# Longformer attention and a gated MLP on one core: later rounds in another unit order, with the second pair's key and query copies behind the first pair's scores

## The chip, the cores and the metric

The kernel runs on one core of one Trainium2 chip. The metric is the device time of the core in microseconds (us); lower is better. A core has the engines TensorE (PE; its weight loads appear as PEld), VectorE (DVE), ScalarE (ACT), GpSimd (POOL) and SyncE (SP, which here issues most of the DMAs). Each engine carries out its instructions in the order written in the program, and waits at an instruction until what that needs is there.

## The reference

Attention over 8 batches, 8 heads, 576 positions and 64 dimensions a head, with a band mask of 32 positions to either side and 8 global positions, which see everything and are seen by everything. The heads are laid side by side to 4608 rows of 512 and go through an MLP whose activation is h·cos(h).

```python
scores = scale * np.matmul(q, k.transpose(0, 1, 3, 2))
mask = np.abs(pos[:, None] - pos[None, :]) <= window        # window = 32
mask = mask | is_global[:, None] | is_global[None, :]
attn = softmax(np.where(mask, scores, -1e9))
x = np.matmul(attn, v)  # heads side by side: (4608, 512)
h = x @ w_in            # (512, 2048)
out = (h * np.cos(h)) @ w_out
```

## The kernel before

The work is cut into pairs of heads (32 pairs: 4 in each of 8 batches) and into half batches of two pairs. The half batch `s` has the pairs `2s` and `2s+1`. For a pair there are, in this order:

- copies: `local_k` (L607, DVE, tile `kw`) and `local_q` (L619, DVE, tile `qb`) spread keys and queries, which a transposing load has put into `kT` and `qT`, into 11 blocks with the room for the global positions in front. POOL fills that room (`globals_kq`, L579 and L586);
- scores: 22 matmuls on PE (L699, tile `st`), which read `kw` and `qb`; then four exponentials on ACT (L702 and L707, tile `e`) and three products with the mask on DVE (L703 and L708, tile `pm`);
- values: 22 matmuls (L719, into `pv`), then four small operations and the normalising product on DVE (L730, tile `xn`);
- turning: 6 transposes on PE (L744, tile `tx`) and two DVE operations, the second of which writes `xT`, the MLP's input; for the last pair of a batch POOL writes the global columns (L752).

The MLP goes over tiles of 512 rows, in units of four matmuls of 128x512 each. An in-unit (L762) makes one block of 128 hidden columns in a bank `ph` of PSUM (two banks take turns, tag "h"; scores use one of them too); ACT takes its cosine (L768) and DVE multiplies (L769), which frees the bank. An out-unit (L800) is a quarter of one output block; four of them fill the bank `po` (one bank, tag "o"), and then ACT or DVE in turn copies it out (L805 or L807) and SP stores it. A cosine and an exponential need different tables on ACT, so each change between them costs a table load (L702 and L768, ACT_TABLE_LOAD).

What stands between what is written out by hand, as strings of steps. A start-up list, `FRONT`, is followed by rounds `s` = 4 to 15, with lists of their own for rounds 4, 5 and 6 (`MID`, `FIFTH`, `SIXTH`), and `ORDER` for the nine rounds 7 to 15. The letters of a step:

- `s`, `p`, `x`: scores, values, turning; `k`, `q`: the copies. The second letter says of which pair: `a` and `z` are the first and second pair of this round's half batch, `c` and `d` the first and second pair of the next round's;
- `1`: an in-unit with its cosine and product; `2`: an out-unit;
- `n`: squares of the previous half batch's `xn` on ACT (L818), for a check of the range;
- `G`: on POOL, the global positions of the next half batch's pairs into `kw` and `qb`, then a copy of one element of this half's `xn` (L980, `gate`), which holds the queue, and then three DMAs that cast values, keys and queries of half batch `s+2` (L268 and L272).

```python
for step in {4: MID, 5: FIFTH, 6: SIXTH}.get(s, ORDER).split():
    if step == "1":
        one()
    elif step == "2":
        two()
    ...
    else:
        f, pr = (STEPS | OTHER)[step[0]], 2 * s + "azcd".index(step[1])
        if pr < B * NP:
            f(pr, *[int(x) for x in step[2:]])
```

At a round's end SP is given the loads for half batch `s+2`: two transposing DMAs into `kT[s % 2]` and `qT[s % 2]` (L284 and L285), and the values. After the last round a tail runs the in- and out-units that are left, one of each in turn. `kw` and `qb` have four buffers each, one per pair, `kT` and `qT` two, one per half batch.

Of the kernel before, what the change touches and what calls it, by code (L numbers as in the profile page):

```python
# [23 lines left out]
G = 8  # L24
# [20 lines left out]
TT = 512  # L45
NTT = NT // TT

ORDER = "sa 2 2 2 2 sz pa 1 1 2 xa pz G 1 1 2 xz n 1 1 2 kc qc 1 kd qd 2 1"

MID = ("+ 1 1 1 1 Z0 1 1 1 Z1 1 1 Z2 1 1 A0 n1 1 Z3 1 1 1 Z4 1 1 A1 n2 1 1 1 Z5 A2 1 1 1 n3 B5 1 2 2 g10 g11 kc qc V10 K6 2 2 1 1 2 2 kd qd - 2 2")  # L50

FIFTH = "sa G 2 2 2 2 sz pa 1 1 2 xa U10 K7 pz 2 2 2 kc qc xz n kd qd"

SIXTH = "sa 2 2 2 2 sz pa 1 1 2 xa pz G 1 1 2 xz n 1 1 D0 2 kc qc D1 1 kd qd D2 2 1"

FRONT = ("M1 s0 E0 C0 E1 L2 k1 q1 w4 s1 y0.0 f4 k2 q2 C1 H0 p0 M2 L3 y0.1 s2 k3 q3 f2 x0 p1 M3 H1 g4 g5 g6 C2 y1.0 s3 g7 L4 I k4 q4 f2 x1 p2 M4 y1.1 s4 "
         "C3 W0 k5 q5 f2 x2 p3 y2.0 s5 g8 g9 W1 W2 W3 k6 q6 f2 x3 p4 y2.1 s6 C4 Y0 k7 q7 f2 x4 p5 n0 y3.0 s7 k8 q8 f2 x5 p6 y3.1 s8 H2 k9 q9 f2 x6 p7 y4.0 s9 "
# [147 lines left out]
def kernel(  # L205
# [694 lines left out]
    with tc.manual_schedule():  # L900
# [107 lines left out]
        for s in range(4, B * NP // 2):  # L1008
            outs_by[0] = 8 * (s - 3)
            for step in {4: MID, 5: FIFTH, 6: SIXTH}.get(s, ORDER).split():  # L1010
                if step == "1":
# [77 lines left out]
```

## Time and profile before

| | |
|---|---|
| time, median of 3 runs | 353.61 us (352.48 to 355.74) |
| profiled execution, span from first to last instruction | 353.2 us (the profile gives no other time of this execution) |
| PE busy | 332.5 us (94%) |
| DVE busy | 250.1 us (71%) |
| ACT busy | 245.9 us (70%) |
| POOL busy | 108.5 us (31%) |
| mean granted PE clock | 0.983 of full speed |
| length of one round with `ORDER` | 17.15 us, nine of them |

Busy time is the time in which an engine works at an instruction; the rest of the span it waits. "Idle before, releaser" in a row is the time that the engine stood still ahead of the instruction, and what ended it. Matmuls overlap, so that a group's length on PE holds a drain that the next group covers; the distance of two starts is what a group costs. A row of the timeline has start, length, engine, line, operation, output and inputs, shape and number of instructions.

### The profile page before, as it was taken

The numbers are of one execution on the slowest core, as the hardware profiler recorded it, in microseconds if no ns is written. First come the engines' busy times: TensorE is split into PE (matmuls) and PEld (weight loads), VectorE is DVE, ScalarE is ACT, GpSimd is POOL, SyncE is SP. The second block draws the span as 40 slices with busy tenths as digits, with TensorE's granted clock in tenths as the row PEclk, the third lists the DMA queues.
The fourth block names the chain that finished last, engine by engine and source line by source line (L and its number), as shares of the span: only waits on it lengthen the run. The fifth ranks groups of instructions, "written<-read, shape, count | busy, mean of one in ns | idle before, by whom it ended". The sixth has DMA issues, their size and how long they took to land.

```text
span 353.2 us, 8389 instructions
## 1 busy us (share of the span) xinstructions
PE 332.5 (94%) x3169; PEld 170.9 (48%) x3169; DVE 250.1 (71%) x611; ACT 245.9 (70%) x423; POOL 108.5 (31%) x221
## 2 busy tenths in 40 slices
PE   7887789999986999999999999999999999999993
PEld 3566675444443444544444545454544444444442
DVE  6565888887586778778787979697878466556410
ACT  8778987884754877777878787777878856644300
POOL 8854847434070507050705071416000100000000
PEclk9898989999999999999999999999999999999998
DMA  5999993999999999999999999999980000100112
GB/s 82 186 149 165 167 192 41 207 164 132 165 147 160 146 199 135 178 118 194 143 187 139 183 139 176 135 161 153 179 93 32 31 32 30 60 32 30 58 63 68
DMA packets 165891, 44.58 MB, mean 126 GB/s; under 512 B 153764, under 2 KB 160996, under 8 KB 165668
## 3 DMA queue, kind: packets, MB, share of 16 engines
q1 hardware_dynamic: 105860, 26.70, 51.2%
q0 software_dynamic: 59984, 17.28, 50.5%
q8 instruction: 27, 0.44, 0.5%
q14 instruction: 20, 0.16, 0.2%
HBM read 44.41 MB, written 19.17 MB: 180 GB/s over the span
## 4 chain that ended last, share of the span: by engine, by line
PE 73%; ACT 8%; DVE 5%; DMA 5%; issue 4%; SPq 3%; POOL 1%; ACTq 0%; POOLq 0%; DVEq 0%
PE po L800 32%; PE ph L762 30%; PE tx L744 2%; DMA kn<-in_k_dram 2%; PE st L699 2%; ACT e L702 2%; PE pv L719 2%; ACT e L634 1%; DMA vw<-vg 1%; ACT e L707 1%; SPq L414 1%; PE po L782 1%; ACT e L638 1%; DVE xn L666 1%; DVE pm L639 1%
## 5 line engine op out<-in xcount | busy, mean ns | idle before, releaser
L762 PE MATMUL ph<-xT,w_in 128*128 128x512 f16 x576 | 140.3, 379 | 1.1 <-DVE g L769 0.3
L768 ACT ACTIVATE cos<-ph,pio 128x512 f16<-128x512 f32 x144 | 97.1, 687 | 62.1 <-PE ph L762 59.9
L800 PE MATMUL po<-w_out,g 128*128 128x512 f16 x560 | 135.4, 379 | 0.0
L769 DVE TENSOR_TENSOR g<-cos,ph 128x512 f16<-128x512 f16 x144 | 95.9, 685 | 42.9 <-ACT cos L768 41.7
L762 PEld LDWEIGHTS <-w_in 128*128 128x128 f16 x576 | 54.2, 97 | 64.6 <-issue 4.6
L800 PEld LDWEIGHTS <-g 128*128 128x128 f16 x560 | 53.7, 98 | 63.6
L703 DVE TENSOR_TENSOR pm<-e,mask 128x512 f16<-128x512 f16 x44 | 18.8, 426 | 19.0 <-ACT e L702 17.7
L702 ACT ACTIVATE e<-st 128x512 f16<-128x512 f32 x44 | 23.9, 594 | 10.0 <-PE st L699 9.8
L980 POOL COPY gate<-xn 1x1 f16<-1x1 f16 x8 | 1.4, 180 | 87.9 <-DVE xn L730 87.9
L752 POOL COPY xT<-xg 128x4 f16 x48 | 15.6, 325 | 32.5 <-DVE xT L747 29.9
L272 POOL DMA_DIRECT2D q<-in_q_dram x11 | 24.0, 2182 | 0.0
L818 ACT ACTIVATE xn<-xn 128x1536 f16<-128x1536 f16 (+1 forms) x16 | 22.5, 1407 | 0.0
L730 DVE TENSOR_TENSOR xn<-pv,r_all 128x768 f16<-128x768 f32 x22 | 21.1, 958 | 1.0
L805 ACT COPY o<-po 128x512 f32<-128x512 f32 x17 | 10.0, 586 | 14.7 <-PE po L800 14.3
L807 DVE COPY o<-po 128x512 f32<-128x512 f32 x18 | 12.4, 690 | 9.0 <-PE po L800 8.5
L272 POOL DMA_DIRECT2D k<-in_k_dram x11 | 18.1, 1645 | 0.9 <-issue 0.9
L768 ACT ACT_TABLE_LOAD x12 | 15.4, 1283 | 0.2
L719 PE MATMUL pv<-vw,pm 128*64 128x65 f16 x484 | 12.7, 197 | 2.7 <-DMA vw<-vg 2.7
L607 DVE COPY kw<-kT 128x1320 f16<-128x1320 f16 x22 | 15.1, 685 | 0.0
L702 ACT ACT_TABLE_LOAD x11 | 14.1, 1283 | 0.2
L699 PEld LDWEIGHTS <-kw 64*128 64x128 f16 x484 | 8.4, 95 | 10.7 <-issue 8.1
L699 PE MATMUL st<-qb,kw 64*128 64x64 f16 x484 | 11.2, 191 | 1.5 <-DVE qb L619 1.1
(185 smaller groups left out, 385.9 us busy)
## 6 DMA issues: line engine op xcount, KB each, us to landing
out_dram<-o SPq DMA_DIRECT2D x35, 256.0 KB
vw<-v SPq DMA_DIRECT2D x32, 165.0 KB
v<-in_v_dram POOLq DMA_DIRECT2D x11, 288.0 KB
k<-in_k_dram POOLq DMA_DIRECT2D x11, 288.0 KB
q<-in_q_dram POOLq DMA_DIRECT2D x11, 288.0 KB
vn<-in_v_dram SPq DMA_DIRECT2D x20, 120.0 KB
w_in<-in_moe_w_in_dram POOLq DMA_DIRECT2D x4, 512.0 KB
w_out<-in_moe_w_out_dram POOLq DMA_DIRECT2D x1, 2048.0 KB
```

What stands on the lines that cost most here:

```text
L272: nc.gpsimd.dma_start(dst[s].rearrange("t (h d) -> t h d", h=4), dview(src, base, (D, S), (S * D, 4), (1, D)))
L699: nc.tensor.matmul(st[j // 8 * 2 + h][:, j % 8 * C : j % 8 * C + C], kp[hp, j], qp[hp, j], start=True, stop=True)
L702: nc.scalar.activation(e[:, 0:512], st[h], AF.Exp, scale=scale)
L703: nc.vector.tensor_tensor(view(pm[:, h], (1, 512)), e[:, 0:512], view(mask, (1, 512)), ALU.mult)
L719: nc.tensor.matmul(pv[r0 : r0 + C, j // 6, c0 : c0 + 65], pm[:, h, j], vp[:, j, h], start=True, stop=True)
L730: nc.vector.tensor_tensor(view(xn, (384, 2), (D, 6), (1, D)), view(pv, (512, 2), (65, 6), (1, D)), view(rp, (6, 2), (1, 6), (0, D)), ALU.mult)
L752: nc.gpsimd.tensor_copy(xT[:, :, bass.ds(pool_idx[g] + b * S, 1)], xg[:, :, g : g + 1])
L762: nc.tensor.matmul(ph, w_in16[:, j, f * P : (f + 1) * P], xT[:, j, t * TT : (t + 1) * TT], start=(j == 0), stop=(j == NC - 1))
L768: nc.scalar.activation(cos, ph, AF.Sin, bias=pio2)
L769: nc.vector.tensor_tensor(g, cos, ph, ALU.mult)
L800: nc.tensor.matmul(po, g16[:, f, s * P : (s + 1) * P], w_out16[:, f], start=(f == 0), stop=(f == NF - 1))
L818: nc.scalar.activation(view(xn, (BP * P, 2), (1, n)), view(xn, (BP * P, 2), (1, n)), AF.Square, accum_out=x_sq[:, s : s + 1])
```

## The change

Two of the hand-written lists change, nothing else. Each round from 7 on does as many in-units (8) and out-units (8) as before, and the same attention work.

- One of the out-units goes to the round's front, ahead of the first pair's scores; three stand between the first and the second pair's scores instead of four.
- The copies of a second pair's keys and queries, so far made near the end of the round before (`kd qd`), are made in the pair's own round, behind the first pair's scores (`kz qz`). Round 6 therefore leaves them out.
- Behind the first pair's values stand in-, out-, in-, out-unit (`1 2 1 2`) instead of two in-units and an out-unit (`1 1 2`).
- The squares (`n`) stand ahead of the second pair's values instead of behind its turning; `G` stands two in-units later. The round ends with two in-units instead of an out-unit and an in-unit.

```diff
-ORDER = "sa 2 2 2 2 sz pa 1 1 2 xa pz G 1 1 2 xz n 1 1 2 kc qc 1 kd qd 2 1"
+ORDER = "2 sa kz qz 2 2 2 sz pa 1 2 1 2 xa n pz 1 1 G 2 xz 1 1 2 kc qc 1 1"
...
-SIXTH = "sa 2 2 2 2 sz pa 1 1 2 xa pz G 1 1 2 xz n 1 1 D0 2 kc qc D1 1 kd qd D2 2 1"
+SIXTH = "sa 2 2 2 2 sz pa 1 1 2 xa pz G 1 1 2 xz n 1 1 D0 2 kc qc D1 1 D2 2 1"
```

The built program's instruction lists differ on PE, DVE and ACT in order alone; those of POOL and SP are the same.

## Prediction

> **What bounds the kernel now.** I read the page first, then busy time by stretches of time, cut at the rounds, then the three engines' timelines of one round.
>
> ```profile
> span 353.2 us, 8389 instructions
> PE 332.5 (94%) x3169; PEld 170.9 (48%) x3169; DVE 250.1 (71%) x611; ACT 245.9 (70%) x423; POOL 108.5 (31%) x221
> ...
> 106.00:123.10 17.10, 14.30 (x153) 7.26 (x152) 12.18 (x27) 10.98 (x21) 5.08 (x9) 1.00 1.39 153
> 123.10:140.25 17.15, 17.09 (x167) 8.38 (x166) 13.96 (x32) 13.07 (x22) 5.38 (x10) 1.00 1.51 167
> ...
> 260.30:277.40 17.10, 17.04 (x147) 8.31 (x146) 12.23 (x28) 13.02 (x22) 2.03 (x10) 1.00 0.13 46
> ```
>
> The columns are length, then busy time (and instructions) of PE, weight loads, DVE, ACT, POOL, then clock. The nine rounds that run the changed list lie between 123.1 and 277.4 us. Each takes 17.15 us and PE is busy for all but 0.06 of it at full clock; DVE has 3 us spare, ACT 4. So PE sets these rounds: a copy on DVE costs nothing there unless PE waits for it, and a wait of PE costs its length. Nine rounds stand or fall together: 0.1 us a round is 0.9 us of the span.
>
> PE through one round (start, length, operation; the length includes a drain that overlaps the next group, so I take starts):
>
> ```profile
> 191.22 0.49 PE L699 MATMUL st<-qb,kw 64*128 64x64 f16 x22
> 191.64 3.63 PE L800 MATMUL po<-w_out,g 128*128 128x512 f16 x16
> 195.20 0.49 PE L699 MATMUL st<-qb,kw 64*128 64x64 f16 x22
> 195.63 0.57 PE L719 MATMUL pv<-vw,pm 128*64 128x65 f16 x22
> 196.13 2.12 PE L762 MATMUL ph<-xT,w_in 128*128 128x512 f16 x8
> 198.09 1.03 PE L800 MATMUL po<-w_out,g 128*128 128x512 f16 x4
> 199.07 0.51 PE L744 MATMUL tx<-ident,xn 128*128 128x128 f16 x6
> 199.51 0.57 PE L719 MATMUL pv<-vw,pm 128*64 128x65 f16 x22
> 200.01 1.90 PE L762 MATMUL ph<-xT,w_in 128*128 128x512 f16 x8
> 201.75 1.03 PE L800 MATMUL po<-w_out,g 128*128 128x512 f16 x4
> 202.61 0.50 PE L744 MATMUL tx<-ident,xn 128*128 128x128 f16 x6
> 203.09 1.89 PE L762 MATMUL ph<-xT,w_in 128*128 128x512 f16 x8
> ```
>
> A unit ("1" or "2", four matmuls) takes 0.86 us (201.75 to 202.61), scores 0.43, values 0.50, transposes 0.44. Little is hidden in this stream: the first pair of in-units takes 1.96 us where the second takes 1.74 (0.22 lost), the out-unit behind it 0.98 for 0.86 (0.12 lost), the second transposes 0.48 for 0.44 (0.04).
>
> What stands between the first pair's scores (191.22) and the second's (195.20) on the other engines:
>
> ```profile
> 191.32 0.69 ACT L768 ACTIVATE cos<-ph,pio 128x512 f16<-128x512 f32 x1 [0.28 <-PE ph L762]
> 192.03 1.28 ACT L702 ACT_TABLE_LOAD   x1
> 193.32 1.08 ACT L702 ACTIVATE e<-st 128x512 f16<-128x512 f32 x2
> 194.29 0.56 ACT L707 ACTIVATE e<-st 128x192 f16<-128x192 f32 x2
> 196.62 0.56 ACT L707 ACTIVATE e<-st 128x192 f16<-128x192 f32 x2
> ...
> 190.92 0.53 DVE L607 COPY kw<-kT 128x1320 f16<-128x1320 f16 x1
> 191.36 0.46 DVE L619 COPY qb<-qT 128x616 f16<-128x616 f16 x1
> 192.04 0.69 DVE L769 TENSOR_TENSOR g<-cos,ph 128x512 f16<-128x512 f16 x1 [0.22 <-ACT cos L768]
> 193.95 0.91 DVE L703 TENSOR_TENSOR pm<-e,mask 128x512 f16<-128x512 f16 x2 [1.22 <-ACT e L702]
> 194.88 0.36 DVE L708 TENSOR_TENSOR pm<-e,mask 128x384 f16<-128x384 f16 x1
> 195.31 0.69 DVE L807 COPY o<-po 128x512 f32<-128x512 f32 x1
> ```
>
> Today the second pair's copies (190.92 and 191.36) end at 191.82, 3.4 us before its scores need them. The first pair's scores go through a chain that begins at the end of the last in-unit: its cosine, the table load, four exponentials, three mask products; DVE leaves it at 195.24.
>
> **The change, part by part.**
>
> *The copies moved.* DVE works in the order written, and in the changed listing kw and qb of the second pair stand directly behind the third mask product. They are two instructions a round: none is added, and the other engines' work is the same in number. But their inputs being ready no longer helps: they start when the chain above is through. The chain does not come earlier. In the new round "1 1 | 2, scores, 2 2 2, scores" as in the old "1 | scores, 2 2 2 2, scores", four out-units and one set of scores lie between the last in-unit's end and the second scores, and the chain hangs on that end (the 0.28 us idle ahead of the cosine is a wait for ph). ACT is idle until then, so the leading out-unit moves the first scores 0.86 us later, inside the 1.28 us table load, and moves nothing earlier.
>
> So, in the clock of the round above: kw and qb follow each other 0.44 us apart (190.92, 191.36), a 0.09 us overlap; with the same overlap behind the product that ends at 195.24, kw starts at 195.15, qb at 195.59, and qb ends at 196.05. For a PE held by this very copy there is one place in the trace, in an earlier round:
>
> ```profile
> 101.58 0.45 DVE L619 COPY qb<-qT 128x616 f16<-128x616 f16 x1
> 102.18 0.67 PE L699 MATMUL st<-qb,kw 64*128 64x64 f16 x22 [1.12 <-DVE qb L619]
> 102.79 3.63 PE L800 MATMUL po<-w_out,g 128*128 128x512 f16 x16
> ```
>
> PE starts 0.15 us after qb's end (102.03), and the 22 matmuls then hold PE for 0.61 us until the next group instead of 0.43. In the new round the second scores start at 196.20 instead of 195.20: 1.00 us late. The slow restart is between 0 and 0.18; I take 0.10, as one row is little. Cost: 1.10 a round, 1.00 to 1.18; if qb's end were felt at once, 0.85.
>
> The Trainium skill, "TensorE: Matmul & The Clock Gate", Part 2 (step by step), says that PE can pull weight loads ahead of running matmuls. By it kw, ready 0.45 us before qb, would be loaded during the wait, the restart would cost nothing and the cost be 1.00. The row at 102.18 speaks against it: kw had been ready there as long, and the restart was slow.
>
> The copies themselves are not slower in the new place if POOL stays out of their way:
>
> ```profile
> L607 DVE COPY kw<-kT x22: 518/527/1832, 82.4 to 259.5; 128x1320 f16<-128x1320 f16 x22
> 206.34 0.81 DVE L607 COPY kw<-kT 128x1320 f16<-128x1320 f16 x1
> 202.57 0.18 POOL L980 COPY gate<-xn 1x1 f16<-1x1 f16 x1 [12.24 <-DVE xn L730]
> ```
>
> The median kw is 0.527 us; 0.81 is seen at the old place while POOL copies xT and issues casts. POOL idles 12.24 us before 202.57, over the new place.
>
> *What is queued behind the copies.* On DVE the output copy (195.31, 0.69) and the second pair's products. The output copy then ends near 196.7; its bank is wanted by the out-unit after scores, values and one in-unit, near 196.20 + 0.43 + 0.50 + 0.86 = 198.0. No new wait.
>
> The first pair's normalised values, xn, and the squares, for the next two parts:
>
> ```profile
> 198.06 0.96 DVE L730 TENSOR_TENSOR xn<-pv,r_all 128x768 f16<-128x768 f32 x1
> 202.54 1.47 ACT L818 ACTIVATE xn<-xn 128x1536 f16<-128x1536 f16 x1
> ```
>
> *"1 1 2" becomes "1 2 1 2" behind the first values.* The second in-unit lost 0.22 us because its bank was freed by the second scores' exponentials (196.62 + 0.56 = 197.18); an out-unit in between covers that. With one unit more, the transposes come 0.86 us later, and 0.43 + 0.50 + 4 x 0.86 = 4.4 us after the second scores, and xn, ending 3.8 us after them (199.02) as now, is there: the 0.12 goes. The second transposes come behind three units as now, but DVE has had PE's delay to catch up, and the 0.04 goes too. Gain: 0.38 a round, at least 0.22, at most 0.42.
>
> *Squares ahead of the second values, casts behind two in-units.* The squares are 1.47 us on ACT: behind them queue the third and fourth cosine, whose inputs come later than the squares end (about 6.2 us after the second scores), and two cosines of 0.69 at 0.86 us spacing are not late. POOL's and SP's instruction order is unchanged; the gate and the three casts hang on xn, which keeps its place relative to the second scores. The key buffer that a later transposing load overwrites is now read until early in its own round instead of the round before, but that load is issued in the round after. Nothing is paid.
>
> *Round six loses the two copies, the end of the last round has "1 1" ahead of the tail's "1".* The first gains nothing (PE bounds). In the second the third in-unit in a row waits for the first one's bank (cosine and product, 0.69 each, against one unit of 0.86): about 0.5 us, of which the tail as it stands loses part already; I take 0.3, from 0 to 0.6.
>
> *Sum.* 1.10 - 0.38 = 0.72 a round; nine rounds 6.5, the tail 0.3: 6.8 us onto the span of 353.2, 360.0. The median of the runs shown, 353.61, is 0.4 above that span, so 360.4. Bounds: 0.85 - 0.42 = 0.43 a round gives 3.9, 1.18 - 0.22 = 0.96 gives 8.6 and the tail 0.6: 357.5 to 362.8.
>
> **The rivals.**
>
> *Faster: the copies find DVE's gap.* DVE idles 1.22 us ahead of the first mask product, and kw and qb need 0.90. Were they to run there, the second scores would start at 195.20 as now and only the 0.38 would remain: 9 x 0.38 = 3.4 less, 350.2. It decides from the point where qb is done by 195.6 (the gain then outweighs the lateness). Against it: the listing has them behind the products, and DVE showed no overtaking in the rows above.
>
> *About as before: the wait is small.* If PE feels qb at once, restarts at full pace and all waits behind it vanish, a round gains 0.43 and the time is 353.6 + 3.9 = 357.5; with kw overlapping the product by 0.15 more, a round loses 0.28 and the time is 353.6 + 2.5 = 356.1. It counts as no change from a loss of 0.39 a round down. For it: the one row of such a wait follows a longer idle stretch than the new one. Against it: that row.
>
> *Dearer: the copies meet POOL.* If the later gate lets POOL's copies and cast issues slide over the new place, kw takes 0.81 (0.28 more) in each round: 9 x 1.00 + 0.3 = 9.3, 362.9. For it: half of the rounds show 0.81 today, at the other place. Against it: the 12.24 us of idle POOL.
>
> *Much dearer: the clock.* PE idle once a round could cost the full clock:
>
> ```profile
> 40.00:60.00 20.00, 17.23 (x257) 11.95 (x257) 16.54 (x49) 16.88 (x34) 12.76 (x31) 0.91 0.79 125
> ```
>
> At 0.91 the 17.1 us of PE work would take 1.7 more: 9 x 1.7 + 6.8 = 22 us, 375.7. Against it: 106.00 to 123.10 has 2.8 us of idle PE, more than the new round, at clock 1.00. The same page of the Trainium skill (Part 1, the second failure mode) tells of a kernel whose short idles between groups of matmuls made the clock swing; no stretch of these rounds shows it.
>
> **How the numbers follow.** The forecast 0.75; dearer by POOL 0.08; clock 0.02; about as before 0.11; faster 0.04. A measurement here tells about 1% (3.5 us) from no change. Slower by over 1% holds the forecast, both dear cases and little of the fourth: 0.85; within 1%: 0.10; faster by over 1%: 0.05 with the chance of something on that side that I do not see. The range reaches from "about as before", 356.1, to the POOL case, 363.0 rounded up.
>
> **What would show it.** Right: a round of 17.8 to 17.9 us; one wait of PE per round, L699 for DVE qb, near 0.9 us; kw starting right behind L708; the first in-units behind the second scores split and no PE wait at L744. Wrong: rounds under 17.5 (the wait is under 0.8, or more was hidden in the stream than I count), kw ahead of L703, kw over 0.7 at the new place, or a clock below 1.00 between 123 and 284 us.

## The result, and the profile after

The changed kernel takes 359.28 us (median, 358.93 to 360.51) against 353.68 for the kernel before: a ratio of 1.0155, with a 95% interval from 1.0127 to 1.0184. Ratios here and below are taken over the fast runs alone (a run is slow when it is over 1.5% above the fastest of its kernel; two runs of the last experiment are) and are not the quotients of the medians. The profiled execution has a span of 358.2 us, 5.0 more than the 353.2 before, and took 359.91 us in all. The head of its page:

```profile
span 358.2 us, 8371 instructions
PE 327.6 (91%) x3169; PEld 171.2 (48%) x3169; DVE 248.8 (69%) x611; ACT 246.1 (69%) x423; POOL 109.2 (30%) x221
```

One round, from first scores to first scores, in busy time by stretches (length, then PE, weight loads, DVE, ACT, POOL, clock):

```profile
194.21:211.82 17.61, 16.72 (x166) 8.47 (x166) 13.73 (x32) 13.07 (x22) 5.53 (x11) 1.00 1.50 154
```

A round is 17.61 us instead of 17.15, at the same full clock, and PE is now idle for 0.89 us of it. PE through that round, in the timeline:

```profile
194.21 0.49 PE L699 MATMUL st<-qb,kw 64*128 64x64 f16 x22
194.63 2.76 PE L800 MATMUL po<-w_out,g 128*128 128x512 f16 x12
198.29 0.50 PE L699 MATMUL st<-qb,kw 64*128 64x64 f16 x22 [0.89 <-issue]
198.72 0.57 PE L719 MATMUL pv<-vw,pm 128*64 128x65 f16 x22
199.22 1.04 PE L762 MATMUL ph<-xT,w_in 128*128 128x512 f16 x4
200.09 1.03 PE L800 MATMUL po<-w_out,g 128*128 128x512 f16 x4
200.95 1.03 PE L762 MATMUL ph<-xT,w_in 128*128 128x512 f16 x4
201.81 1.03 PE L800 MATMUL po<-w_out,g 128*128 128x512 f16 x4
202.68 0.50 PE L744 MATMUL tx<-ident,xn 128*128 128x128 f16 x6
203.11 0.57 PE L719 MATMUL pv<-vw,pm 128*64 128x65 f16 x22
...
206.21 0.50 PE L744 MATMUL tx<-ident,xn 128*128 128x128 f16 x6
206.54 1.89 PE L762 MATMUL ph<-xT,w_in 128*128 128x512 f16 x8
```

The idle time stands at one place, ahead of the second pair's scores (198.29). The units behind the first values (199.22 to 202.68) are 0.86 to 0.87 us apart, with no loss. DVE ahead of the wait in the timeline, and, in the second block, the row of PE's list of waits (us in total, times, longest):

```profile
196.08 0.91 DVE L703 TENSOR_TENSOR pm<-e,mask 128x512 f16<-128x512 f16 x2 [1.22 <-ACT e L702]
197.01 0.36 DVE L708 TENSOR_TENSOR pm<-e,mask 128x384 f16<-128x384 f16 x1
197.29 0.53 DVE L607 COPY kw<-kT 128x1320 f16<-128x1320 f16 x1
197.73 0.46 DVE L619 COPY qb<-qT 128x616 f16<-128x616 f16 x1
198.11 0.68 DVE L807 COPY o<-po 128x512 f32<-128x512 f32 x1
```

```profile
PE st L699 <- issue: 8.0, 9, 0.9
```

The copy of the queries ends at 198.19 and the scores begin 0.10 us later. The list of waits names no engine ("issue"), though: that it is the copies is shown by the experiments, not by this row.

The 5.0 us of span lie as follows. Up to the last in-unit ahead of the first changed round the execution after is 0.27 us later (121.93 against 121.66), in a part where the two kernels are the same but for the two copies that round six leaves out. The nine rounds, counted from the end of that unit to the end of the last round's last in-unit, take 158.52 us against 154.34, 4.18 more, 0.46 a round. The tail takes 0.54 more.

### The profile page after: what moved, and what is told of

The parts are those of the page before. It is cut to its first block, busy times and chain, and to the rows that moved or that the text cites. A ratio compares the mean times of both kernels' runs of the same rounds, so it can differ in the third digit from the quotient of the medians.

```text
span 358.2 us, 8371 instructions
## 1 busy us (share of the span) xinstructions
PE 327.6 (91%) x3169; PEld 171.2 (48%) x3169; DVE 248.8 (69%) x611; ACT 246.1 (69%) x423; POOL 109.2 (30%) x221
## 4 chain that ended last, share of the span: by engine, by line
PE 77%; DMA 6%; ACT 5%; issue 4%; DVE 3%; SPq 2%; POOL 1%; ACTq 0%; POOLq 0%; DVEq 0%
PE ph L762 33%; PE po L800 32%; PE pv L719 3%; PE st L699 3%; DMA kn<-in_k_dram 2%; DMA vw<-vg 2%; PE tx L744 2%; DMA vn<-in_v_dram 1%; PE pv L646 1%; ACT e L638 1%; PE bank L595 1%; ACT e L634 1%; PE po L782 1%; SPq L373 1%; SPq L357 1%
## 5 line engine op out<-in xcount | busy, mean ns | idle before, releaser
L800 PE MATMUL po<-w_out,g 128*128 128x512 f16 x560 | 136.8, 379 | 0.0
L607 DVE COPY kw<-kT 128x1320 f16<-128x1320 f16 x22 | 13.8, 629 | 0.0
```

The lines of the kernel that those rows point to most:

```text
L800: nc.tensor.matmul(po, g16[:, f, s * P : (s + 1) * P], w_out16[:, f], start=(f == 0), stop=(f == NF - 1))
```

## The experiments

The theory: PE waits for copies that stand behind the first pair's mask products on DVE, about 0.96 us a round, and the new unit order itself saves about 0.50 of it. Rivals: the unit order costs the time; reading keys and queries a round later holds up the transposing loads; the wait has a fixed price, whatever is copied there. Under each heading stands the edit to the list `ORDER`, with `SIXTH` made to fit.

**The copies ahead of the first pair's scores in the same round (changed kernel otherwise)**

```diff
-"2 sa kz qz 2 2 2 sz pa 1 2 1 2 ..."
+"kz qz 2 sa 2 2 2 sz pa 1 2 1 2 ..."
```

> The changed kernel with the second pair's copies moved from behind the first pair's scores to the head of the same round; PE's, ACT's, POOL's and SP's order stay. Theory (the second scores wait for copies that stand behind the first pair's mask products): the wait of about 0.9 us a round at the second scores is gone, a round falls from 17.61 us to about 16.65, and the time to about 350.5 us, below the kernel before. Rival one (the new unit order itself costs the time): rounds stay at 17.6 and the time near 359. Rival two (keys and queries read a round later hold up the transposing loads): the same, 17.6 and 359, since the copies still read them in their own round.

Measured: 349.38 us, ratio to the kernel before 0.9887 (0.984 to 0.9934). A round of it in busy time by stretches, and in the timeline PE and DVE at the second scores of the next:

```profile
187.67:204.32 16.65, 16.65 (x165) 8.44 (x164) 13.82 (x32) 13.07 (x22) 5.51 (x11) 1.00 1.43 159
```

```profile
204.75 2.76 PE L800 MATMUL po<-w_out,g 128*128 128x512 f16 x12
207.45 0.49 PE L699 MATMUL st<-qb,kw 64*128 64x64 f16 x22
...
204.89 0.53 DVE L607 COPY kw<-kT 128x1320 f16<-128x1320 f16 x1
205.35 0.45 DVE L619 COPY qb<-qT 128x616 f16<-128x616 f16 x1
206.20 0.91 DVE L703 TENSOR_TENSOR pm<-e,mask 128x512 f16<-128x512 f16 x2 [0.40 <-ACT e L702]
```

The wait is gone, all eight distances between rounds are 16.65 us, and the kernel is faster than both. PE's instructions are the same in the same order as in the changed kernel; only two copies on DVE have moved in front of three products. So the copies' place costs 17.61 - 16.65 = 0.96 us a round, and neither the unit order nor the later reading does. The copies now run in the 1.22 us for which DVE used to wait for the first exponential; 0.40 of it is left.

**The copies back at the end of the round before**

```diff
-"2 sa kz qz 2 2 2 sz ... xz 1 1 2 kc qc 1 1"
+"2 sa 2 2 2 sz ... xz 1 1 2 kc qc 1 kd qd 1"
```

> The changed unit order with the copies back at the end of the round before (round six too). Theory: the round is 16.65 us as with the copies ahead, span about 349.5. Rival one (the unit order costs): 17.6. Rival two (the later reading costs): 16.65 here and 17.6 with the copies ahead in their own round.

Measured, one run: 348.54 us, span 346.7, rounds of 16.65 (the first 16.74). The rounds are the same as with the copies ahead: it does not matter in which round they are made, only that they are ahead of the products.

**The order before, with only the copies moved**

```diff
-"sa 2 2 2 2 sz ... xz n 1 1 2 kc qc 1 kd qd 2 1"
+"sa kz qz 2 2 2 2 sz ... xz n 1 1 2 kc qc 1 2 1"
```

> The order before with only the copies moved behind the first pair's scores. Theory: the second scores come 0.96 us later each round and none of the 0.50 us that the new unit order saves is saved, so 17.15 + 0.96 = 18.1 us a round, 8.6 us on nine rounds, time near 362. Rival (the delay at the second scores also lets the later waits of the round vanish, whatever the units' order): 17.6 to 17.7 a round and 358.5.

Measured: 362.96 us, ratio 1.0242 (1.0184 to 1.03). PE in the timeline:

```profile
199.73 0.50 PE L699 MATMUL st<-qb,kw 64*128 64x64 f16 x22 [0.90 <-issue]
200.16 0.57 PE L719 MATMUL pv<-vw,pm 128*64 128x65 f16 x22
200.66 2.11 PE L762 MATMUL ph<-xT,w_in 128*128 128x512 f16 x8
202.60 1.03 PE L800 MATMUL po<-w_out,g 128*128 128x512 f16 x4
203.59 0.51 PE L744 MATMUL tx<-ident,xn 128*128 128x128 f16 x6
...
207.13 0.50 PE L744 MATMUL tx<-ident,xn 128*128 128x128 f16 x6
207.61 1.89 PE L762 MATMUL ph<-xT,w_in 128*128 128x512 f16 x8
```

Rounds are 18.08 to 18.10 us, 0.95 over the 17.15 before, as the theory has it and not the rival. The waits behind the first values stay (200.66 to 202.60 is 1.94, 202.60 to 203.59 is 0.99), since they hang on the second scores and are late with them. So the two parts of the change add: 0.95 lost by the copies, 0.49 won by the order (18.10 to 17.61).

**Half the dose: only the queries' copy behind the first scores**

```diff
-"2 sa kz qz 2 2 2 sz ... xz 1 1 2 kc qc 1 1"
+"2 sa qz 2 2 2 sz ... xz 1 1 2 kc qc 1 kd 1"
```

> The changed kernel with the keys' copy back in the round before, and only the queries' copy behind the first pair's scores: half the dose. Theory (PE waits for the end of the last copy in line behind the mask products): the wait falls by the 0.44 us that the keys' copy takes on DVE, 17.61 to 17.17 us a round, span about 354. Rival (a fixed price for any wait there, such as a restart): the round stays above 17.4.

Measured, one run: 357.11 us, span 355.4. Seven of eight rounds take 17.18 to 17.22 us, as the theory has it; one takes 18.25, with a 0.8 us wait of the values for a DMA in the list of waits; with this round the span is longer than the 354 expected. PE and DVE in the timeline, and a row of the list of waits:

```profile
196.11 0.50 PE L699 MATMUL st<-qb,kw 64*128 64x64 f16 x22 [0.46 <-issue]
196.54 0.56 PE L719 MATMUL pv<-vw,pm 128*64 128x65 f16 x22
...
195.54 0.47 DVE L619 COPY qb<-qT 128x616 f16<-128x616 f16 x1
```

```profile
PE st L699 <- DVE qb L619: 2.0, 4, 0.5
```

In five of the nine rounds the wait falls from 0.89 to 0.46 us, by 0.43, the time that kw kept DVE. In the four others it is 0.50, and there the list of waits names the releaser itself: DVE, qb. A fixed price is out.

**Where the saving of the order comes from: the spread units alone**

```diff
-"sa 2 2 2 2 sz pa 1 1 2 xa pz ... kc qc 1 kd qd 2 1"
+"sa 2 2 2 2 sz pa 1 2 1 2 xa pz ... kc qc 1 kd qd 1"
```

> The order before with one edit: in-, out-, in-, out-unit behind the first values instead of two in-units and an out-unit (the out-unit at the round's end moves there). Theory (this one edit makes the whole saving: the second in-unit no longer waits for its bank, the first transposes no longer for xn, and with one unit more ahead of them the second transposes neither): 0.50 us a round less, 16.65 instead of 17.15, time near 349.5. Rival (the second transposes are relieved by the squares' move or by the copies' late place): 16.8 or more.

Measured: 354.41 us, ratio 0.9974 (0.9943 to 1.0006), rounds mostly of 17.05 to 17.11. The expectation of 16.65 was wrong, and not for the rival's reason. PE in the timeline:

```profile
191.18 0.43 PE L699 MATMUL st<-qb,kw 64*128 64x64 f16 x17
191.89 0.24 PE L699 MATMUL st<-qb,kw 64*128 64x64 f16 x5 [0.27 <-DVE g L769]
192.06 3.63 PE L800 MATMUL po<-w_out,g 128*128 128x512 f16 x16
...
200.01 0.50 PE L744 MATMUL tx<-ident,xn 128*128 128x128 f16 x6
200.44 0.57 PE L719 MATMUL pv<-vw,pm 128*64 128x65 f16 x22
...
203.54 0.50 PE L744 MATMUL tx<-ident,xn 128*128 128x128 f16 x6
203.87 1.89 PE L762 MATMUL ph<-xT,w_in 128*128 128x512 f16 x8
```

The whole saving behind the second scores is there: both transposes go unhindered, 0.43 and 0.33 us as in the changed kernel. But the out-unit that moved had stood between the round's last two in-units. Now the first scores' fourth bank is one that an in-unit has just filled, and the last five of 22 matmuls wait for its product on DVE; the scores take 0.88 us (191.18 to 192.06) instead of 0.42. The saving of about 0.5 is spent on these scores, which take 0.46 us longer, 0.27 of it plain idleness. In the changed kernel the out-unit at the round's front stands in that place.

**The squares alone, and the leading out-unit alone**

```diff
-"sa 2 2 2 2 sz pa 1 1 2 xa pz G 1 1 2 xz n 1 1 2 ..."
+"sa 2 2 2 2 sz pa 1 1 2 xa n pz G 1 1 2 xz 1 1 2 ..."
```

> The order before with only the squares moved ahead of the second values. Theory: ACT's place for them matters to nobody, 17.15 us a round as before, or a little more, since with the out-unit still at its old place the third in-unit's cosine now queues behind them. Rival (the squares' move pays a part of the saving): 17.0 or less.

Measured, one run: 354.74 us, span 353.0, rounds 17.14 to 17.15 but for one of 17.57, in which the second pair's values wait for a DMA. The squares' place matters to nobody.

```diff
-"sa 2 2 2 2 sz ..."
+"2 sa 2 2 2 sz ..."
```

> The order before with only one out-unit moved from between the two sets of scores to ahead of the first. Theory: the chain of cosine, table load, exponentials starts at the last in-unit's end and four out-units still lie behind it, so nothing moves: 17.15 us a round. Rival (three units between the scores are too few for the banks of the first scores): the second scores wait, 17.3 or more.

Measured, one run: 354.94 us, span 353.2, rounds 17.14 to 17.15. By itself the leading unit does nothing; it is worth something only together with the spread units, where the bank wait is gone (17.10 against 16.65 with the leading unit, the squares and the casts moved as well). That it is the leading unit and not the squares or the casts that takes it away was not run apart.

**One more out-unit ahead of the tail (copies ahead of the scores)**

```diff
         tail[0] = True
+        two()
         for i in range(NTT * NF):
```

> The copies ahead of the first pair's scores in their own round, and one out-unit more ahead of the tail, so that no three in-units stand in a row at the seam. Theory: the 0.6 us wait of an in-unit for its bank at the tail's start goes, rounds stay at 16.65, time near 348.8, the fastest of the kernels. Rival (the wait moves to the next in-unit, behind the squares on ACT): nothing gained over 349.4.

Measured: 352.39 us (median of six, 348.05 to 354.10), ratio to the kernel before 0.9875 (0.9811 to 0.9939). This run was beside another group of runs of the kernel before (median 355.14; 354.31 beside the copies ahead), so ratios are to be compared, and they do not differ from the copies ahead (0.9887). The seam in the timeline, without the unit (copies ahead) and, in the second block, with it:

```profile
268.24 1.89 PE L762 MATMUL ph<-xT,w_in 128*128 128x512 f16 x8
270.77 1.04 PE L762 MATMUL ph<-xT,w_in 128*128 128x512 f16 x4 [0.64 <-DVE g L769]
```

```profile
272.69 1.89 PE L762 MATMUL ph<-xT,w_in 128*128 128x512 f16 x8
274.41 1.03 PE L800 MATMUL po<-w_out,g 128*128 128x512 f16 x4
275.27 1.03 PE L762 MATMUL ph<-xT,w_in 128*128 128x512 f16 x4
```

The wait of 0.64 us is gone and none takes its place there. As a time that is too small to be told here: where the rounds begin scatters more (the first scores of the changed rounds at 121.07 us in the copies ahead, at 125.52 here). In this profiled execution a transposing load of the queries came late, before the changed rounds, and PE stood still for longer than in the other profiles, where it waits 1.11 or 1.12 us at this place:

```profile
104.35 0.75 PE L699 MATMUL st<-qb,kw 64*128 64x64 f16 x22 [2.87 <-DVE qb L619]
105.04 5.08 PE L800 MATMUL po<-w_out,g 128*128 128x512 f16 x16
```

The granted clock was 0.50 behind that pause (105.10 to 108.00 us), and the 16 matmuls took 5.01 us to the next group instead of 3.56 in the copies ahead. That the pause brought the clock down is not shown by one execution.

## Why the prediction was right, and where it was off

- *PE sets the rounds, and a wait costs its length:* shown. 0.95 to 0.96 us more or less ahead of the second scores is as much on the round, with either unit order.
- *The chain does not come earlier, the copies start when it is through:* right. From the last in-unit's cosine to the second scores the sum had 4.88 us (196.20 - 191.32); in the changed kernel it is 4.84 (198.29 - 193.45).

```profile
193.45 0.69 ACT L768 ACTIVATE cos<-ph,pio 128x512 f16<-128x512 f32 x1 [0.18 <-PE ph L762]
```

- *Cost of the wait, 1.10 us a round:* too high, 0.96. The second scores start 0.10 us after qb's end, not 0.15, and the slow restart is not there at all (198.29 to 198.72 is the usual 0.43). That term was taken from one row at 102.18 us. The sentence beside it came nearer: by the rule of the Trainium skill ("TensorE: Matmul & The Clock Gate", Part 2) that weight loads are pulled ahead, the prediction had a restart that costs nothing and a wait of 1.00. But pulling ahead is not the reason: the weight loads of these scores start at 198.26, 0.44 us after kw's end and only once qb is there too, and in the round before that the prediction shows they start together with the scores, though kw had long been ready. Changed kernel, then before:

```profile
198.26 0.41 PEld L699 LDWEIGHTS <-kw 64*128 64x128 f16 x22 [1.36 <-issue]
```

```profile
195.20 0.38 PEld L699 LDWEIGHTS <-kw 64*128 64x128 f16 x22 [0.42 <-issue]
```

- *Gain of the order, 0.38, at most 0.42:* too low, 0.50. From the second scores to the in-units behind the second transposes it took 7.89 us (203.09 - 195.20); now it takes 8.25 (206.54 - 198.29) with one unit of 0.86 more, so 0.50 less. The 0.22 and the 0.12 came as worked out. The second transposes gave 0.15 instead of 0.04, 0.33 us instead of 0.48: I had taken the first transposes' 0.44 for the unhindered price, but these stand ahead of values (0.43 in the changed kernel too, 202.68 to 203.11), the second ones ahead of an in-unit. And the reason given, that DVE catches up during PE's wait, is refuted from both sides: with the copies ahead PE waits for nothing and the 0.15 is there, and in the order before with only the copies moved PE waits as long and the second transposes still take 0.48 (207.13 to 207.61). With one more unit ahead of the second values, DVE is less far behind when they come: xn ends 2.41 us after they start (203.11 to 205.52) instead of 2.94 (199.51 to 202.45). Before, and in the second block the changed kernel:

```profile
201.49 0.96 DVE L730 TENSOR_TENSOR xn<-pv,r_all 128x768 f16<-128x768 f32 x1
202.50 0.44 PEld L744 LDWEIGHTS <-xn 128*128 128x128 f16 x6 [0.22 <-DVE xn L730]
```

```profile
204.56 0.96 DVE L730 TENSOR_TENSOR xn<-pv,r_all 128x768 f16<-128x768 f32 x1
205.99 0.54 PEld L744 LDWEIGHTS <-xn 128*128 128x128 f16 x6
```

  Before, xn ended 0.16 us ahead of the transposes (202.45, 202.61), and their weight loads had to wait for it. Now it ends 0.69 us ahead (205.52, 206.21), and the loads start 0.22 us before the transposes, while the out-unit still runs.
- *The rest:* POOL stayed away from the new place (kw 0.53 us). The 0.81 us of the rival "dearer by POOL" was a misreading: the copy at 206.34 is the first pair's (`kc`), and in the kernel before the nine copies of a second pair's keys from 122.32 us on took 0.53 or 0.54 (208.07: 0.53). The clock stayed at 1.00, the squares cost nothing. The tail cost 0.54 instead of 0.3.
- *The signs:* a round of 17.61 us lies below the 17.8 to 17.9 named as the sign of being right, and above the 17.5 named as the sign of being wrong. The others came: one wait of 0.89 us a round at the second scores (though the profile calls it "issue"), kw right behind L708, the in-units split, no wait at the transposes.
- *The sum:* 9 x 0.46 = 4.2, tail 0.5 and start 0.3 make 5.0 on the span against 6.8 forecast. The median moved by 5.6. Cost and gain were both missed to the same side, by 0.14 and 0.12 us a round, 2.3 us on nine rounds; the tail and the start gave 0.5 of it back. The forecast median, 360.4, is only 1.1 too high, and that is in part luck: the span was put 1.8 too high, but what lies around it, 0.4, was taken from another execution's span and is too low; the profiled execution of the changed kernel took 1.7 over its own.
- *The rival "faster":* its mechanism is real, as the kernel with the copies ahead shows: its price was put at 350.2 us, and that kernel takes 349.38. The changed kernel just does not do it.

## What to carry to other kernels

On an engine that works in order, an instruction whose inputs are ready should stand ahead of one that waits for another engine, not behind it: two copies of 0.9 us that cost nothing in a gap of 1.22 us cost 0.96 us each round behind it. A reordering can hold a gain and a loss at once, so separate the edits: here one part won 0.5 us a round, another lost 0.96, and undoing only the second made the kernels that were fastest here. And spreading units changes who uses a bank next: a unit taken from one seam was worth as much there as where it went.

## What the runs showed that I had not expected

- A PE that is "busy" for 17.09 of 17.15 us was not at its bound: with the same matmuls in another order the round takes 16.65 us, still fully busy in the profile. 0.50 us of waits had been counted as busy time, and showed only in the distances between starts.
- The wait of PE for DVE's copies is named "issue" in nine rounds of the changed kernel and "DVE qb" in four of the rounds with half the dose. The name is not to be relied on for this wait.
- After 0.46 and 0.89 us of idleness PE took up the scores at full pace (0.43 us), while after 1.12 us, at the place early in the program that the prediction used, they took 0.61. The granted clock does not tell them apart: it was 1.00 there too (102.10 to 102.85 us). What makes the difference, the length of the pause or the place, stays open.
